# Attention steps on a fixed plan: one burst behind each second product instead of two paced streams

## The chip, the core and the metric

The kernel runs on one core of a Trainium2 chip. The metric is the time of one execution on the device, in microseconds (us); lower is better. Five engines work side by side, each through its own list of instructions in order: PE (TensorE, matrix products and transposes), DVE (VectorE), ACT (ScalarE), POOL (GpSimd) and SP (SyncE, which here issues nearly all DMA transfers). PE writes only to the accumulator memory PSUM, and DVE or ACT must empty a PSUM buffer before PE can use it again.

## The reference

Attention over 4 batches, 8 heads, 576 positions, 64 features per head, with two kinds of causal mask; then two MLPs over the 2304 tokens of width 512.

```python
mask_local = (rel >= 0) & (rel < 32)                       # heads 0 to 3
mask_strided = (rel >= 0) & (pos[None, :] % 32 == pos[:, None] % 32)   # heads 4 to 7
attn = softmax(where(mask, scale * q @ k.T, -1e9));  x = attn @ v       # -> (2304, 512)
h = x @ w_in;  r = np.maximum(h, 0.0);  x = (s * (r * r) + b) @ w_out   # d_ff = 2048
return ((x @ w_a) * (x @ w_b)) @ w_out2                                 # d_ff = 1536
```

## The kernel before

The tokens are cut into six blocks of 384 (`TB`), n = 0 to 5. For each block the first MLP runs over f = 0 to 15, slices of 128 hidden features. One iteration f has a **first product** `h_mm(n, f)` (12 matmuls of 128x384 into the PSUM tile `h`), whose result ACT and DVE turn into `gt`, and a **second product** `o_mm` for the slice two iterations back (12 matmuls into the four PSUM tiles `acc`). Every product is written as three passes over a high and a low half, so operands have a hi part (written by ACT) and a lo part (written by DVE, from the hi part).

A block's input tile `x` comes from attention, worked out while the block before it is in the MLP: during block n PE also does the attention of block n+1. Block 0's own attention (`first`) stands ahead of the loop. In block 0 DVE and ACT also convert the weights from raw words, one pair (`w_in`, `w_out`) per iteration, in `next_weights`; in blocks 1 to 4 they convert the second MLP's weights (`convert_w2`), which POOL stores to DRAM.

The attention of a block is four **local** generators (`local`, a pair of heads and 192 positions each) and two **strided** generators (`strided`, a pair of heads, in two halves); for block 1 it is four `strided_one` instead. A generator is a chain of steps separated by `yield`. The names in the trace, in the order of the chain:

- local: `pqk` (transposes of q and k; eight ACT copies into `qz` and `kT`), `pss` from `kT,qz` (scores), the softmax on `lpt` (DVE reduces and masks, ACT takes the exponentials, and a step later DVE normalises), `ppt` from `lpt` (transpose; ACT copies it to `pT`), `po` from `pT,vn` (output; ACT and DVE write it to `x`).
- strided: `pst` (transposes of q and k), `pss` from `skT,sqT`, softmax on `spt`, `ppt` from `spt`, `po` from `spT,sv`. `strided_one` is the same with the tile names `spo` and `spTo`.

The small tiles (`qn`, `kn`, `vn`, `kT`, `lpt`, `sk`, `sv`, ...) have one buffer each, and the attention's PSUM tiles share the three buffers of `ps_a`.

What sets the order: `in_order` chains every step's instructions behind PE's last one, so **PE's order is that of the code**. The other engines' lists are ordered by the framework's own scheduling, under that constraint. Two `Stream` objects, one for the local chain and one for the strided chain, are called twice in each iteration, once behind the first product and once behind the second (lines 810 to 816). A stream has a rate, steps divided by calls (line 701: `2 + 7 * len(gens)` steps, line 791: `2 * NF1 - 4` calls), and makes a step whenever a whole one is due; `overlapped` begins the next generator when the one before it is at its third or fourth step. So the places of the steps follow from the rates, and the two chains drift against each other.

At a block's end the four `acc` tiles are copied out by ACT (`o1s`, in three buffers shared with `r` and with each other) and stored by SP; the next block's second product needs those `acc` tiles from f = 2 on. When block 5 begins, the attention's pools are closed and SP loads the second MLP's first weights (`w` from `w2d`) and its input (`xr` from `o`, line 615) into the same memory. Some matmuls `pb` of the second MLP are then put between those of block 5.

Of the kernel before, what the change touches and what calls it, by code (L numbers as in the profile page):

```python
# [26 lines left out]
def sparse_attention_two_mlps(  # L27
# [28 lines left out]
    HL = H // 2  # L56
# [3 lines left out]
    TU = QT * NJ  # L60
# [4 lines left out]
    NB = NT // TB  # L65
    NT2 = TB // P
    KD = DM // P
    NF1 = FF1 // P
# [49 lines left out]
    @contextmanager  # L118
    def after(instructions):
        with ExitStack() as st:  # L120
            for i in instructions:
                st.enter_context(tc.issue_after(i))
            yield

    def in_order(step, *args):

        with after(list(last_pe)):
            return step(*args)
# [103 lines left out]
    def local(spans, n, hp_, c0):  # L232
# [39 lines left out]
        for j, (bb, t0) in enumerate(spans):  # L272
            nc.sync.dma_start(
                out=vn[:, j], in_=v[bb, hs, t0 - STR:t0 + QT, :].rearrange("h t d -> t h d")
            )
        yield
        pss = ps_a.tile([QT, 2, NJ, P], F32, tag="a", name="pss")
# [8 lines left out]
        yield from softmax(pt, [pss[:, i] for i in range(2)], mask[:, None, None, :].to_broadcast([QT, 2, NJ, P]))  # L286
        yield
        yield
# [104 lines left out]
    def strided(bb, pair):  # L393
# [29 lines left out]
        )  # L423
        yield
        half = S // QT // 2
# [6 lines left out]
        for g, r0 in enumerate(R0):  # L432
            for h in range(2):
# [3 lines left out]
                )  # L437
        yield
        kr = kT.rearrange("p (i r) -> p i r", r=STR)
        for g0, g1 in ((0, 3), (3, len(R0))):  # L440
# [11 lines left out]
            yield from softmax(pt, pss, smask[:, None, None, :].to_broadcast([NQ, 2, ng, NK]))  # L452
            yield
            yield
# [28 lines left out]
    def strided_one(pair, i):  # L483
# [22 lines left out]
        for j in range(2):  # L506
            for h in range(2):
# [3 lines left out]
                )  # L511
        yield
        pss = [ps_a.tile([QT, 2, TU], F32, tag="a", name="pss") for _ in range(2)]
        for j in range(2):
            for h in range(2):
                t = kqT[h * D:(h + 1) * D, 3 * j * QT:(3 * j + 3) * QT]
                mm(pss[h][:, j], lhsT=t[:, TU:], rhs=t[:, 0:TU], start=True, stop=True)
        pt = sp.tile([P, 2 * 3 * P], F32, tag="spt", name="spo")[:QT].rearrange("p (h j c) -> p h j c", h=2, j=2)
        yield from softmax(pt, pss, omask[:, None, None, :].to_broadcast([QT, 2, 2, TU]))
        yield  # L520
        yield
# [149 lines left out]

    def drain(gen):
        for _ in gen:
            pass

    class Stream:
# [10 lines left out]

    def overlapped(gens, at):

        next(gens[0])  # L690
        yield
        yield
        for i, g in enumerate(gens):
            for step, _ in enumerate(g):
                if step == at and i + 1 < len(gens):
                    next(gens[i + 1])
                yield

    def local_gens(n):
        if n == 1:  # L700
            spans = [[(2 * i, QT), (2 * i + 1, QT)] for i in range(2)]
        else:
            spans = [[(n - 2, p * TU), (n - 2, p * TU + QT)] for p in range(1, NP)]
        gens = [local(sp_, n, hp_, i * TU) for i, sp_ in enumerate(spans) for hp_ in range(HL // 2)]
        return overlapped(gens, 3), 2 + 7 * len(gens)

    def strided_gens(n):
        if n == 1:
            gens = [strided_one(pair, i) for i in range(2) for pair in range(2)]
            return overlapped(gens, 3), 2 + 7 * len(gens)  # L710
        gens = [strided(n - 2, pair) for pair in range(2)]
        return overlapped(gens, 4), 2 + 13 * len(gens)

# [61 lines left out]
    gens = [first(bb, qks[bb], vs[bb], fmask, *banks[bb]) for bb in range(B)]  # L775
    live, step = list(range(B)), 0
# [4 lines left out]
    for _ in range(EARLY):  # L781
        next_weights()
    later = [
        Stream(convert_w2(), 3 * NF2 + 1, (NB - 2) * NF1 - 2), Stream(column_sums(), NF1 + 1, 2 * NF1 - 1)
    ]
    queue = []
    for n in range(NB):
        acc = [ps_acc.tile([P, TB], F32, tag="acc", name="acc") for _ in range(KD)]
        if n + 1 < NB:

            streams = [Stream(*g(n + 1), 2 * NF1 - 4) for g in (local_gens, strided_gens)]
        else:
            streams = []
            att.close()
            p2 = ctx.enter_context(tc.tile_pool(name="p2", bufs=1, reuse_waits="tile"))
            wx = ctx.enter_context(tc.tile_pool(name="wx", bufs=NX, reuse_waits="tile"))
            for i in range(NX):
                load_w2(i)
            x2n = load_x2(0)
        for f in range(NF1):  # L800
            order = ExitStack()
            if n == 0:
                if len(wi) < NF1 and f:

                    with after(behind):
                        next_weights()

                order.enter_context(tc.issue_after(first_done[B - 1].ins))
            gt = in_order(h_mm, n, f)
            for st in streams:  # L810
                st()
            queue.append((acc, gt, f, n))
            if len(queue) > AHEAD1:
                in_order(o_mm, *queue.pop(0))
            for st in streams:
                st()
            order.close()
            if n == NB - 1:
                while len(w2) < NX + 2 * (f + 1 - AHEAD1):
                    load_w2(len(w2))  # L820
            elif n:
                for st in later[:n]:
                    st()
        for st in streams:
            drain(st.gen)
    for item in queue:
# [47 lines left out]
```

## Time and profile before

| | |
|---|---|
| median of 3 runs | 1040.44 us (1040.05 to 1041.5) |
| the profiled execution, its own time | 1042.37 us |
| the profiled execution, its span in the trace | 1040.5 us |
| PE busy | 997.3 us (96%) |
| weight loads of PE (PEld) busy | 936.0 us (90%) |
| DVE busy, ACT busy | 470.0 us (45%), 461.7 us (44%) |
| mean granted TensorE clock | 0.988 of full speed |

The span falls into stages: before the first `h` (to 39.4 us), block 0 (39.4 to 154 us), blocks 1 to 4 (154 to 511 us), block 5 and the second MLP (511 to 1040.5 us). In the timeline a row gives the start, the duration from the first to the last instruction of the group, the engine, line, tiles and count, and in brackets the idle time of the engine just before and what ended it. Matmuls overlap in the records, so what a group costs on PE is read from its start to the next group's start, not from its duration.

### The profile page before, as it was taken

Reading aid. Unit: us, or ns where it says so; the run is one execution under the profiler, and the core shown is the slowest. Engines: PE = TensorE matmul, PEld = TensorE weight load, DVE = VectorE, ACT = ScalarE, POOL = GpSimd, SP = SyncE. Lnnn points to the kernel's source line nnn. Section 1 sums busy time; section 2 is a strip of 40 time slices with the busy share of each in tenths; the row PEclk is TensorE's granted clock in tenths of the full one; section 3 lists DMA queues with packets and bytes.
Section 4 is the critical chain, followed back from the end, with each engine's and each line's share of the span. In section 5 each row is a group of like instructions: output and inputs, shape, how many; then the busy total and the mean of one; then the engine's idle time right before and its main releaser. Section 6 shows DMA issues by size and latency. Waiting matters only on the chain.

```text
span 1040.5 us, 15811 instructions
## 1 busy us (share of the span) xinstructions
PE 997.3 (96%) x5984; PEld 936.0 (90%) x5984; DVE 470.0 (45%) x1246; ACT 461.7 (44%) x1291; POOL 72.6 (7%) x110
## 2 busy tenths in 40 slices
PE   6878979999999899999999999999999999999998
PEld 5768979999899899889999989999999999999997
DVE  5689755766878677576522221211211211211111
ACT  6677846665675666567532231311311311211212
POOL 3000000001233132100000000000000000000000
PEclk9988989999999999999999999999999999999999
DMA  9556422456454554644567710200200100000000
GB/s 190 190 185 183 152 56 78 144 157 195 142 142 136 175 138 139 194 140 148 192 196 252 249 32 2 61 1 1 61 1 1 61 1 1 31 1 1 31 1 30
DMA packets 109819, 106.37 MB, mean 102 GB/s; under 512 B 59568, under 2 KB 94640, under 8 KB 109744
## 3 DMA queue, kind: packets, MB, share of 16 engines
q1 hardware_dynamic: 104560, 86.49, 28.9%
q0 software_dynamic: 5184, 18.88, 4.8%
q8 instruction: 47, 0.77, 0.3%
q14 instruction: 28, 0.23, 0.1%
HBM read 77.03 MB, written 28.31 MB: 101 GB/s over the span
## 4 chain that ended last, share of the span: by engine, by line
PE 85%; DVE 6%; ACT 5%; DMA 3%; issue 1%; SPq 0%; ACTq 0%; DVEq 0%
PE acc L113 30%; PE h L113 18%; PE pb L113 14%; PE pa L113 14%; PE pss L113 2%; PE po L113 2%; PE ppt L116 2%; DMA o<-o1s 1%; DMA xr<-o 1%; PE fss L113 1%; DVE raw L160 1%; DVE w L132 1%; DVE raw L163 1%; DVE raw L157 1%; ACT r L560 1%
## 5 line engine op out<-in xcount | busy, mean ns | idle before, releaser
L113 PE MATMUL h<-x,w 128*128 128x384 f32 x1152 | 229.2, 348 | 3.4 <-DVE w L132 1.3
L113 PE MATMUL acc<-gt,w 128*128 128x384 f32 x1152 | 223.0, 341 | 3.2 <-ACT o1s L586 3.2
L113 PEld LDWEIGHTS h<-x,w 128*128 128x128 f32 x1152 | 205.4, 194 | 7.9 <-DVE w L132 1.6
L113 PEld LDWEIGHTS acc<-gt,w 128*128 128x128 f32 x1152 | 199.4, 189 | 7.4 <-ACT o1s L586 3.8
L641 DVE TENSOR_TENSOR ab<-pb,ab 128x384 f32<-128x384 f32 x72 | 40.1, 557 | 306.7 <-ACT ab L640 306.7
L113 PE MATMUL pb<-x,w 128*128 128x384 f32 x864 | 165.0, 337 | 0.0
L113 PE MATMUL pa<-x,w 128*128 128x384 f32 x864 | 162.1, 335 | 1.5 <-ACT ab L640 1.5
L113 PE MATMUL acc<-w,abt 128*128 128x512 f32 x648 | 161.8, 393 | 0.0
L640 ACT ACTIVATE ab<-pa 128x384 f32<-128x384 f32 x72 | 35.4, 491 | 282.4 <-PE pa L113 282.3
L113 PEld LDWEIGHTS pb<-x,w 128*128 128x128 f32 x864 | 153.6, 188 | 6.4 <-DVE x L132 0.3
L113 PEld LDWEIGHTS pa<-x,w 128*128 128x128 f32 x864 | 150.8, 188 | 2.6 <-ACT ab L640 2.5
L113 PEld LDWEIGHTS acc<-w,abt 128*128 128x128 f32 x648 | 120.5, 188 | 21.9
L560 ACT ACTIVATE r<-h 128x384 f32<-128x384 f32 x96 | 46.8, 488 | 115.6 <-PE h L113 115.3
L567 DVE TENSOR_TENSOR r<-r 128x384 f32<-128x384 f32 x80 | 48.8, 610 | 91.1 <-ACT gt L566 90.5
L132 DVE TENSOR_TENSOR abt<-ab,abt 128x384 fp32r<-128x384 f32 x72 | 40.2, 558 | 46.8 <-ACT abt L131 46.8
L131 ACT ACTIVATE w<-raw 128x512 fp32r<-128x512 f32 x68 | 44.8, 670 | 25.7 <-DVE raw L163 21.6
L568 DVE TENSOR_TENSOR gt<-r,gt 128x384 fp32r<-128x384 f32 x80 | 54.1, 676 | 4.5
L132 DVE TENSOR_TENSOR w<-raw,w 128x512 fp32r<-128x512 f32 x68 | 45.9, 685 | 21.7 <-ACT w L131 20.8
L131 ACT ACTIVATE abt<-ab 128x384 fp32r<-128x384 f32 x72 | 37.7, 524 | 40.2 <-DVE ab L641 40.2
L604 POOL DMA_DIRECT2D w2d<-w x36 | 20.0, 556 | 431.6 <-DVE w L132 358.9
L163 DVE SCALAR_TENSOR_TENSOR raw<-raw 128x512 uint32<-128x512 uint32 x68 | 46.5, 686 | 0.7
L160 DVE SCALAR_TENSOR_TENSOR raw<-raw 128x512 uint32<-128x512 uint32 x68 | 45.9, 685 | 0.5
(109 smaller groups left out, 878.7 us busy)
## 6 DMA issues: line engine op xcount, KB each, us to landing
w2d<-w POOLq DMA_DIRECT2D x36, 512.0 KB, 5.2
w<-w2d SPq DMA_DIRECT2D x36, 512.0 KB
raw<-in_moe_w_out_dram SPq DMA_DIRECT2D x28, 512.0 KB
raw<-in_moe_w_in_dram SPq DMA_DIRECT2D x16, 512.0 KB
raw<-in_moe_w_a_dram SPq DMA_DIRECT2D x12, 512.0 KB
raw<-in_moe_w_b_dram SPq DMA_DIRECT2D x12, 512.0 KB
xr<-o SPq DMA_DIRECT2D x6, 768.0 KB
o<-o1s SPq DMA_DIRECT2D x20, 192.0 KB
```

The source lines that it names most:

```text
L113: last_pe[:] = [nc.tensor.matmul(*args, **kwargs).ins]
L116: last_pe[:] = [nc.tensor.transpose(*args).ins]
L131: nc.scalar.activation(out=hi, in_=src, func=AF.Copy)
L132: return eng_lo.tensor_tensor(out=lo, in0=src, in1=hi.bitcast(F32), op=ALU.subtract)
L160: nc.vector.scalar_tensor_tensor(out=low, in0=high, scalar=3, in1=low, op0=ALU.logical_shift_left, op1=ALU.bitwise_or)
L163: nc.vector.scalar_tensor_tensor(out=high, in0=high, scalar=0x80000000, in1=low, op0=ALU.bitwise_and, op1=ALU.bitwise_or)
L560: relu = nc.scalar.activation(out=r, in_=ph, func=AF.Relu)
L567: nc.vector.tensor_tensor(out=r, in0=r, in1=r, op=ALU.mult)
L568: lo = nc.vector.tensor_tensor(out=gt[:, 1], in0=r, in1=gt[:, 0].bitcast(F32), op=ALU.subtract)
L604: stores.append(nc.gpsimd.dma_start(out=w2d[i - 1], in_=w.bitcast(F32)).ins)
L640: nc.scalar.activation(out=ab, in_=pa, func=AF.Copy)
L641: nc.vector.tensor_tensor(out=ab, in0=pb, in1=ab, op=ALU.mult)
```

## The change

The streams, `overlapped` and the pacing by rate go. `plan(n)` lists for every generator the iteration numbers at which it makes its next step, and `attend(number)` makes all steps of one number. `attend` is called once per iteration, behind the second product; in the first three iterations of block 0, where steps would come too late, also behind the first product, and three numbers are called ahead of the loop. Numbers run on over the blocks, so the steps of one block's attention begin up to six iterations before the block in front of it and end in that block's last iteration.

```diff
-    def overlapped(gens, at):
-        next(gens[0])
...
+    steps = {}
+    def plan(n):
         if n == 1:
             spans = [[(2 * i, QT), (2 * i + 1, QT)] for i in range(2)]
+            far = [(4 * i - 3, strided_one(i % 2, i // 2), (-2, 0, 1, 2, 3, 4)) for i in range(4)]
         else:
             spans = [[(n - 2, p * TU), (n - 2, p * TU + QT)] for p in range(1, NP)]
+            far = [(8 * i - 3, strided(n - 2, i), (-3, 0, 1, 2, 3, 4, 4, 5, 6, 7)) for i in range(2)]
+        near = [
+            (4 * i - 1, local(spans[i // 2], n, i % 2, i // 2 * TU), (-2, 0, 1, 2, 3, 4)) for i in range(4)
+        ]
+        for first_, gen, at in near + far:
+            for t in at:
+                steps.setdefault((n - 1) * NF1 + first_ + t, []).append(gen)
+    def attend(number):
+        for gen in steps.pop(number, []):
+            in_order(next, gen)
...
             gt = in_order(h_mm, n, f)
-            for st in streams:
-                st()
+            if n == 0 and f < 3:
+                attend(2 * f - 3)
             queue.append((acc, gt, f, n))
             if len(queue) > AHEAD1:
                 in_order(o_mm, *queue.pop(0))
-            for st in streams:
-                st()
+            attend(n * NF1 + f if n or f > 2 else 2 * f - 2)
```

To fit, some `yield` lines go: the load of v is now in the step of the scores, the strided transposes of q and of k are one step, and of the two empty steps between the normalising and the transpose `ppt` one goes. The same instructions run; nothing in the work of a step changes.

PE at the start of block 0, before (`pss` from `skT` and `spo` belong to `strided_one`):

```order
L113 MATMUL h<-x,w 128x384 x24
L116 MATMUL pqk<-ident,qn 128x96 x2
L116 MATMUL pqk<-ident,kn 128x128 x2
L116 MATMUL pst<-ident,sk 128x96 x6
L113 MATMUL h<-x,w 128x384 x12
L113 MATMUL pss<-kT,qz 96x128 x4
L113 MATMUL pss<-skT 96x192 x4
L113 MATMUL acc<-gt,w 128x384 x12
L113 MATMUL h<-x,w 128x384 x12
L113 MATMUL acc<-gt,w 128x384 x12
L116 MATMUL ppt<-ident,lpt 128x96 x4
L116 MATMUL ppt<-ident,spo 96x96 x8
```

The same place after:

```order
L113 MATMUL h<-x,w 128x384 x12
L116 MATMUL pst<-ident,sk 128x96 x6
L113 MATMUL pss<-skT 96x192 x4
L113 MATMUL h<-x,w 128x384 x12
L116 MATMUL pqk<-ident,qn 128x96 x2
L116 MATMUL pqk<-ident,kn 128x128 x2
L113 MATMUL pss<-kT,qz 96x128 x4
L116 MATMUL ppt<-ident,spo 96x96 x8
L113 MATMUL h<-x,w 128x384 x12
L113 MATMUL po<-spTo,sv 64x96 x8
```

The strided chain has moved ahead of the local one and both begin earlier; transposes and the scores that read them now stand next to each other with no product between.

PE in block 1, iterations 5 to 7, before:

```order
L113 MATMUL h<-x,w 128x384 x12
L113 MATMUL pss<-skT,sqT 84x126 x4
L113 MATMUL acc<-gt,w 128x384 x12
L113 MATMUL pss<-kT,qz 96x128 x4
L113 MATMUL h<-x,w 128x384 x12
L113 MATMUL acc<-gt,w 128x384 x12
L116 MATMUL ppt<-ident,spt 126x84 x4
L113 MATMUL h<-x,w 128x384 x12
L116 MATMUL ppt<-ident,lpt 128x96 x4
L113 MATMUL po<-pT,vn 64x96 x4
L113 MATMUL po<-spT,sv 64x84 x4
L113 MATMUL acc<-gt,w 128x384 x12
```

PE in block 1, iterations 2 to 4, after:

```order
L113 MATMUL h<-x,w 128x384 x12
L113 MATMUL acc<-gt,w 128x384 x12
L116 MATMUL ppt<-ident,lpt 128x96 x4
L113 MATMUL h<-x,w 128x384 x12
L113 MATMUL acc<-gt,w 128x384 x12
L113 MATMUL po<-pT,vn 64x96 x4
L116 MATMUL pqk<-ident,qn 128x96 x2
L116 MATMUL pqk<-ident,kn 128x112 x2
L116 MATMUL ppt<-ident,spt 126x84 x4
L113 MATMUL h<-x,w 128x384 x12
L113 MATMUL acc<-gt,w 128x384 x12
L113 MATMUL pss<-kT,qz 96x128 x4
```

Before, `po` stands right behind the `ppt` it depends on; after, a whole pair of products lies between any two dependent steps. A block of 16 iterations has 23 such bursts before and 16 after, and no burst after uses more than three PSUM tiles of `ps_a`.

## Rows read from the trace of the kernel before

**Rows 1.** Busy time by stretch: us, then PE, PEld, DVE, ACT, POOL, clock, DMA.

```profile
39.40:154.00 114.60, 97.14 (x609) 90.37 (x610) 88.34 (x230) 82.14 (x218) 0.00 (x0) 0.91 0.47 144
70.40:142.80 72.40, 63.50 (x427) 59.58 (x426) 63.21 (x166) 57.18 (x156) 0.00 (x0) 0.90 0.44 131
154.00:511.00 357.00, 347.07 (x2401) 327.88 (x2400) 247.70 (x706) 228.67 (x728) 62.93 (x68) 1.00 0.50 149
```

**Rows 2.** Waits of PE in blocks 1 to 4: us in total, times, longest.

```profile
PE po L113 <- ACT pT L293: 3.6, 4, 1.2
PE acc L113 <- ACT o1s L586: 3.2, 2, 2.6
PE pst L116 <- ACT kT L267: 1.9, 4, 0.8
```

**Rows 3.** PE timeline in block 1, where nothing waits.

```profile
169.03 0.94 PE L113 MATMUL pss<-skT,sqT 64*84 64x126 f32 x12
169.90 2.38 PE L113 MATMUL h<-x,w 128*128 128x384 f32 x12
172.11 2.24 PE L113 MATMUL acc<-gt,w 128*128 128x384 f32 x12
174.19 0.49 PE L116 MATMUL ppt<-ident,lpt 96*128 96x96 f32 x4
```

**Rows 4.** ACT timeline: weight scaling in block 0, and four copies of transposes.

```profile
45.12 1.21 ACT L153 ACTIVATE raw<-raw 128x512 f32<-128x512 f32 x2
...
335.82 1.03 ACT L267 ACTIVATE qz<-pqk 64x96 f32<-64x96 f32 x4
```

**Rows 5.** PE timeline at the beginning of block 3.

```profile
346.20 0.79 PE L113 MATMUL acc<-gt,w 128*128 128x384 f32 x3 [2.59 <-ACT o1s L586]
...
348.41 3.22 PE L113 MATMUL h<-x,w 128*128 128x384 f32 x12
```

**Rows 6.** ACT and DVE timelines behind the last local output of block 4.

```profile
504.79 0.33 ACT L131 ACTIVATE x<-po 128x192 fp32r<-128x192 f32 x1
...
505.15 0.36 DVE L132 TENSOR_TENSOR x<-po,x 128x192 fp32r<-128x192 f32 x1 [0.95 <-ACT x L131]
```

**Rows 7.** Waits of the SP queue.

```profile
SPq L273 <- PE po L113: 93.3, 15, 12.0
```

**Rows 8.** Waits of PE in block 0.

```profile
PE ppt L116 <- DVE lpt L223: 7.6, 2, 5.4
PE ppt L116 <- DVE spo L223: 2.7, 1, 2.7
PE po L113 <- ACT pT L293: 2.0, 1, 2.0
PE po L113 <- DVE spTo L529: 1.4, 1, 1.4
PE h L113 <- DVE w L132: 1.3, 1, 1.3
PE pss L113 <- ACT kT L267: 1.1, 1, 1.1
```

**Rows 9.** PE timeline in block 0, at two of its waits.

```profile
69.23 1.49 PE L116 MATMUL ppt<-ident,spo 96*96 96x96 f32 x8 [2.69 <-DVE spo L223]
70.42 3.90 PE L113 MATMUL h<-x,w 128*128 128x384 f32 x12
...
140.88 0.87 PE L116 MATMUL ppt<-ident,lpt 96*128 96x96 f32 x4 [5.41 <-DVE lpt L223]
...
142.94 3.53 PE L113 MATMUL h<-x,w 128*128 128x384 f32 x12
```

**Rows 10.** Input of the second MLP: SP and ACT timelines, then the chain of waits.

```profile
504.78 0.37 SPq L615 DMA_DIRECT2D xr<-o  x1
...
516.16 2.14 ACT L620 ACTIVATE xr<-xr,b_col 128x384 f32<-128x384 f32 x4 [2.37 <-DMA w<-w2d]
...
604.27 4.46 DMA xr<-o
```

More of the change, by code (lines that the diff above doesn't have):

```diff
@@ L275, in local @@
             )
-        yield
         pss = ps_a.tile([QT, 2, NJ, P], F32, tag="a", name="pss")
@@ L286, in local @@
         yield from softmax(pt, [pss[:, i] for i in range(2)], mask[:, None, None, :].to_broadcast([QT, 2, NJ, P]))
-        yield
         yield
@@ L423, in strided @@
         )
-        yield
         half = S // QT // 2
@@ L437, in strided @@
                 )
-        yield
         kr = kT.rearrange("p (i r) -> p i r", r=STR)
@@ L452, in strided @@
             yield from softmax(pt, pss, smask[:, None, None, :].to_broadcast([NQ, 2, ng, NK]))
-            yield
             yield
@@ L511, in strided_one @@
                 )
-        yield
         pss = [ps_a.tile([QT, 2, TU], F32, tag="a", name="pss") for _ in range(2)]
@@ L519, in strided_one @@
         yield from softmax(pt, pss, omask[:, None, None, :].to_broadcast([QT, 2, 2, TU]))
-        yield
         yield
@@ L669, in token @@
         return (n - 2) * S + TU + c, TB
-    def drain(gen):
-        for _ in gen:
-            pass
     class Stream:
@@ L686, in __call__ @@
                 self.due -= 1.0
-    def overlapped(gens, at):
-        next(gens[0])
[L691 to L699, printed above, removed]
+    steps = {}
+    def plan(n):
         if n == 1:
             spans = [[(2 * i, QT), (2 * i + 1, QT)] for i in range(2)]
+            far = [(4 * i - 3, strided_one(i % 2, i // 2), (-2, 0, 1, 2, 3, 4)) for i in range(4)]
         else:
             spans = [[(n - 2, p * TU), (n - 2, p * TU + QT)] for p in range(1, NP)]
[L704 to L712, printed above, removed]
+            far = [(8 * i - 3, strided(n - 2, i), (-3, 0, 1, 2, 3, 4, 4, 5, 6, 7)) for i in range(2)]
[8 more added lines that the diff above has]
+            in_order(next, gen)
     AHEAD1, AHEAD2, EARLY = 2, 1, 3
@@ L785, in sparse_attention_two_mlps @@
     ]
+    for n in range(1, NB):
+        plan(n)
+    for number in (-6, -5, -4):
+        attend(number)
     queue = []
@@ L788, in sparse_attention_two_mlps @@
         acc = [ps_acc.tile([P, TB], F32, tag="acc", name="acc") for _ in range(KD)]
[L789 to L793, printed above, removed]
+        if n + 1 == NB:
+            assert not steps
             att.close()
@@ L823, in sparse_attention_two_mlps @@
                     st()
-        for st in streams:
-            drain(st.gen)
     for item in queue:
```

## The prediction, as it was made before the run

> **What bounds the kernel now.** I read the busy times by stretch first, then the waits of PE in each stretch, then the timelines around the longest of them. In blocks 1 to 4 PE works 347.1 of 357.0 us, at full clock, while DVE and ACT are busy 248 and 229 us [rows 1]: PE is the bound, and what a new order can give back there is the 9.9 us of idle PE and the price of switching between attention and products. Block 0 is another regime: PE 97.1 us, DVE 88.3 and ACT 82.1 us in 114.6 us, at a mean granted clock of 0.91 [rows 1]. Three engines are nearly full and wait for each other. From 511 us on there is no attention, and PE works nearly all the time; there I expect no gain.
>
> **Blocks 1 to 4, part by part.** *The waits.* 3.6 us are `po` waiting for ACT to copy `pT` [rows 2]: that happens where `ppt` and `po` stand in one burst. After the change 12 + 12 matmuls lie between them, two times 2.08 us by the starts of [rows 3] (172.11 to 174.19), against about half a microsecond for the copy. This wait goes, and so do 1.9 us of `pst` waiting for a PSUM buffer behind the copies of `kT` [rows 2], since no burst takes more than the three buffers and the next one comes 4.2 us later. In that time ACT has to make eight copies, of which four take 1.03 us [rows 4], so some 2.1 us of 4.2; together with the relu, the square and the weights there is still room. About 1.2 us of the 9.9 are small waits of other kinds, and they go with the spacing. The last 3.2 us are `acc` waiting at a block's beginning for the copies `o1s` [rows 2]. What ends them is a store out of the three shared buffers, and nothing in the plan speaks to that; it also cost clock: the `h` behind it lasted 3.22 us [rows 5] against 2.38 [rows 3], and the three matmuls and twelve scores ahead of that `h` took 2.2 us (346.20 to 348.41) instead of some 1.4; together 1.6 us. I count all 11.5 us as gone and put new waits against them: `o1s` again, between 0 and 4.2 us (2.6 + 1.6, its dearest case [rows 5]) at each of four block ends, and the new wait at a block's end. There the last local output now stands in the last iteration, right before the next block's first `h`, which reads it. The chain behind it is 0.33 us on ACT and 0.36 us on DVE, 0.72 us from 504.79 to 505.51 [rows 6], and the hand-over from PE; the transposes `pqk` behind it, some 0.4 us, and the first three matmuls of `h`, 0.5 us, cover most of that, so about 0.2 us if ACT and DVE are free and up to 1 us if not. Behind a waiting `h` everything on PE is queued. Together I take 4 us for the new waits, with ends 1 and 17.
>
> *The bursts.* The product behind a burst takes 2.21 us (169.90 to 172.11), the one behind a product 2.08 us (172.11 to 174.19) [rows 3]. That is 0.13 us per burst. Blocks 1 to 4 have 92 bursts before and 63 after (block 4 has one without): 29 x 0.13 = 3.8 us, take 4, with ends 2 and 6.
>
> *Work moved.* Transposes, six score pairs (169.03 to 169.90, 0.87 us [rows 3]) and `pqk` that began a block's attention now run in the block before: block 4 loses about 1.9 us, block 0 gains them.
>
> *The other queues.* A step carries its loads with it. Before, SP stood 93.3 us behind loads of v that waited for `po` to free the buffer [rows 7], with the weights and the stores of `o1s` queued behind them; after, `po` has read it an iteration earlier and SP passes. I count nothing for that, but it is the reason not to take the upper end for `o1s`. POOL's stores wait for DVE as before.
>
> Sum for blocks 1 to 4: -11.5 - 4 - 1.9 + 4 = **-13.4 us**.
>
> **Block 0.** *Its beginning.* The waits on PE up to 70.4 us are 2.2 (a part of the 7.6), 2.7, 1.3 and 1.1 us [rows 8], 7.3 in all. In their place come two chains with nothing in between. Behind `pst` the scores wait for a copy that stands on ACT behind the relu and two weight scalings of 1.21 us [rows 4]: about 1.2 us. Behind `pqk` the local scores wait for the eight copies, 2.1 us, and in ACT's list relu, square and weights stand among them: between 2.1 and 5.3 us, and I take 4.9, since all of those stand ahead. Those pieces then run at half clock, as the eight `ppt` at 69.23 did (1.19 us to the next start); some 2.3 us more. 4.9 + 1.2 + 2.3 - 7.3: **+1 us**, with ends -3 and +5.
>
> *The rest.* From 70.4 us PE waits 2.0 + 1.4 + 5.4 us [rows 8], and each longer wait costs clock behind it: `h` lasted 3.90 us at 70.42 and 3.53 us at 142.94 [rows 9], against 2.38 [rows 3]. That makes some 12 us that could come back. But the weights must be converted: from 70.4 to 142.8 us, where the last one is ready, DVE was busy 63.2 of 72.4 us [rows 1], so the last weight cannot come more than 9 us earlier, and each engine still waits for another now and then. The softmax now has a whole iteration more before `ppt` reads it, which is what the 5.4 us lacked. I take **-8 us**, ends -12 and +3. The moved work adds 1.9, fewer bursts take 1 off. Block 0: +1 - 8 + 0.9 = **-6 us**.
>
> **Block 5.** The last local output comes one iteration later against the block's beginning, and the load of `xr` waits for it. Before, it was issued at 504.78 and used at 516.16, behind 2 MB of weights [rows 10]; after, those weights wait for the strided tiles only, which are free three iterations earlier, and `xr` alone lands in 4.46 us [rows 10]. `pb` stands where it stood, behind the second iteration's `acc`. I take **+1 us**, ends 0 and +8.
>
> **Sum:** -13.4 - 6 + 1 = -18.4. The profiled execution took 1042.37 us with a span of 1040.5, 1.9 us around it; it would take 1024.0. Against the median of the runs, 1040.44, that is **1022 us**.
>
> **Rivals.** (a) *Block 0 gives nothing.* DVE's weights stay the bound there and every gap closed on PE opens as a wait for a weight: then -13.4 + 1 give **1028**. For it: DVE 63.2 of 72.4 us; against it: PE waited once for a weight in the whole block, 1.3 us [rows 8]. Chance 0.12. (b) *Block ends.* `o1s` costs 4.2 us at each of four ends [rows 5]: 17 instead of 4, **1035**. For it: the plan does not touch its cause, and exponentials now stand in ACT's list beside the copies; against it: in two of the four ends it cost nothing before. Chance 0.06. (c) *The input of the second MLP* is late: if `xr` again needs 11.4 us, but from the beginning of block 5, the `pb` matmuls wait and the products behind them too, +8: **1029**. Chance 0.04. (d) *The clock.* The bursts gather transposes, and their rows show no loss so far: clock 1.00 in blocks 1 to 4 [rows 1], where six to nine transposes and small score groups already stood before a product. If a burst left the clock at its lower level, 1.2 GHz, the `h` behind it would take 3.2 instead of 2.2 us [rows 5]; for the seven bursts of nine transposes plus their neighbours about 8 us: **1030**. The Trainium skill, TensorE: Matmul & The Clock Gate, Part 4 (PE-mode transpose), says that transposes do not count as activity of PE for the clock in the way matmuls do, which speaks for this rival; the clock of 1.00 here does not bear it out. Chance 0.03. (e) *Slower.* In block 0 a burst uses all three PSUM buffers, and the next one needs them 4.2 us of products later. If DVE, with the weights in its list, is later than that with the reduce of the scores, PE waits in every burst until the thirteenth: 13 waits of 2.0 us, like the one for `pT` [rows 8], are 26 us, and nothing of the 8 us comes back: -13.4 + 1 + 0.9 + 26 + 1 = +15.5 give **1056** at worst; without the 26 the sum is -10.5, so it decides for slower from 10.5 / 13 = 0.8 us per burst. For it: DVE is 87% busy in that stretch [rows 1]; against it: before, PE never waited there for a reduce [rows 8]. With some 1.1 us per burst it is 1044. Chance 0.12, a quarter of it within the noise. That the change does not do what it says is excluded by the order of PE's instructions.
>
> **How the numbers follow.** The forecast (1010 to 1027) has 0.63; (a) to (d) have 0.25 and are faster too; (e) has 0.12. A difference of under 0.2% (2 us) is about what a measurement here cannot tell from no change. Faster 0.87, within it 0.04 (0.03 of (e), 0.01 of (b)), slower 0.09. For the range I leave out (e) and the lowest 0.05 of the forecast: 1010 to 1035.
>
> **What would show it.** Right: blocks 1 to 4 in some 343 us with `po`-behind-`pT` and `pst`-behind-`kT` gone from the waits of PE; block 0 in about 108 us, with a wait of several us for `kT` near its beginning and no 5 us wait for `lpt`; block ends with waits of under 1 us for `x`. Wrong: waits of PE for a reduce of `mx` or for weights in block 0, waits for `o1s` at every block end, a granted clock under 1.00 in blocks 1 to 4, or `pb` or `h` waiting for `xr` at the beginning of block 5.

## The result, and the profile after

The changed kernel takes 1023.84 us (median of 4 runs, 1022.7 to 1027.23) where the kernel before took 1040.24 us beside it: 0.985 of the time, 95% interval 0.9826 to 0.9874, 16.4 us less. The prediction was 1022 us. Run again later, on a chip where the kernel before took 1040.1 us, it took 1024.1 us: 0.9849 (0.983 to 0.9868). The profiled execution took 1023.17 us with a span of 1021.4 us, against 1042.37 and 1040.5 us.

The blocks are told apart by where each block's first `h` begins in PE's timeline. The table gives the profiled executions, and the sums that the prediction had made.

| stretch | before, us | after, us | difference | predicted |
|---|---|---|---|---|
| block 0 | 114.5 | 106.1 | -8.4 | -6 |
| blocks 1 to 4 | 86.55 + 87.82 + 93.80 + 88.91 = 357.1 | 85.13 + 87.77 + 89.16 + 85.32 = 347.4 | -9.7 | -13.4 |
| block 5 and the second MLP | 529.5 | 528.6 | -0.9 | +1 |
| sum | | | -19.0 | -18.4 |

The sum was nearly right and its parts were less so. The first view is busy time by stretch, as in [rows 1] with its columns (us, PE, PEld, DVE, ACT, POOL, clock, DMA): first of the kernel before with the cuts at the blocks' first `h`, then of the changed kernel.

```profile
39.45:153.94 114.49, 97.08 (x608) 90.31 (x609) 88.23 (x230) 82.14 (x218) 0.00 (x0) 0.91 0.47 143
153.94:511.02 357.08, 347.15 (x2401) 327.96 (x2401) 247.78 (x706) 228.67 (x728) 62.93 (x68) 1.00 0.50 149
511.02:1040.50 529.48, 523.20 (x2785) 493.28 (x2784) 109.42 (x201) 123.92 (x250) 0.00 (x0) 1.00 0.17 54
```

```profile
39.36:145.44 106.08, 95.90 (x634) 88.36 (x634) 91.17 (x245) 84.48 (x233) 0.00 (x0) 0.97 0.52 158
145.44:492.82 347.38, 341.85 (x2378) 324.37 (x2377) 251.55 (x689) 225.57 (x713) 63.30 (x68) 1.00 0.52 154
492.82:1021.40 528.58, 522.96 (x2786) 493.41 (x2784) 109.50 (x201) 124.47 (x251) 0.00 (x0) 1.00 0.16 53
```

PE's idle time, the stretch less PE's busy time, fell from 17.4 to 10.2 us in block 0 and from 9.9 to 5.5 us in blocks 1 to 4. In block 0 PE issued 26 matmuls more and in blocks 1 to 4 23 fewer: that is the first attention of block 2, which moved forward. It is counted among what blocks 1 to 4 save and what block 0 must carry.

PE's waits after, in us, times and the longest, which answer to [rows 8] (block 0) and to [rows 2] (blocks 1 to 4). First block 0:

```profile
PE pss L113 <- ACT kT L267: 4.9, 1, 4.9
PE ppt L116 <- DVE lpt L223: 2.2, 1, 2.2
PE pss L113 <- ACT skT L387: 1.0, 1, 1.0
PE pst L116 <- ACT sqT L419: 1.0, 1, 1.0
...
```

and blocks 1 to 4:

```profile
PE h L113 <- ACT r L553: 4.0, 4, 1.8
PE h L113 <- DVE x L132: 1.1, 2, 0.7
PE h L113 <- ACT x L131: 0.2, 1, 0.2
```

No wait for `pT`, none of `pst` for a buffer behind `kT` and none of `acc` for `o1s` is left. The 5.4 us wait for `lpt` near the end of block 0 [rows 9] is gone. What is there instead is one long wait at the beginning of block 0, for `kT`, and waits of `h` for the relu `r`, a kind that the prediction had not named.

The 1.0 us of `pst` corrects the description of the change, which says that no burst takes more than three PSUM tiles of `ps_a`. One does, in block 0, where the last steps of block 1's attention meet the first of block 2's: the output `po`, the transposes `pst` of q and the two halves of those of k want four tiles, and the last half waits until ACT has copied `sqT` out of one. PE's timeline:

```profile
131.83 0.93 PE L113 MATMUL po<-spTo,sv 96*64 96x96 f32 x16
132.70 0.55 PE L116 MATMUL pst<-ident,sq 128*128 128x128 f32 x3
133.08 0.41 PE L116 MATMUL pst<-ident,sk 96*128 96x96 f32 x3
134.45 0.47 PE L116 MATMUL pst<-ident,sk 96*128 96x96 f32 x3 [0.96 <-ACT sqT L419]
```

### The profile page after: what moved, and what is told of

Its sections match the earlier page's. It is cut to its first block, busy times and chain, and to the rows that moved or that the text cites. A ratio compares the mean times of both kernels' runs of the same rounds, so it can differ in the third digit from the quotient of the medians.

```text
span 1021.4 us, 15787 instructions
## 1 busy us (share of the span) xinstructions
PE 990.5 (97%) x5984; PEld 930.6 (91%) x5984; DVE 476.8 (47%) x1246; ACT 461.6 (45%) x1291; POOL 73.0 (7%) x110
## 4 chain that ended last, share of the span: by engine, by line
PE 72%; ACT 10%; DVE 10%; DMA 4%; issue 2%; POOL 0%; SPq 0%; ACTq 0%; POOLq 0%; DVEq 0%
PE acc L113 25%; PE pb L113 14%; PE pa L113 14%; PE h L113 13%; DVE gt L561 2%; DMA w2d<-w 2%; DVE raw L160 2%; PE pss L113 2%; ACT w L131 1%; ACT raw L153 1%; DVE w L132 1%; DMA o<-o1s 1%; DVE raw L157 1%; ACT spt L216 1%; DMA xr<-o 1%
## 5 line engine op out<-in xcount | busy, mean ns | idle before, releaser
L113 PE MATMUL acc<-gt,w 128*128 128x384 f32 x1152 | 215.6, 334 | 0.0
L113 PEld LDWEIGHTS h<-x,w 128*128 128x128 f32 x1152 | 200.7, 191 | 15.4 <-ACT r L553 5.4
L561 DVE TENSOR_TENSOR gt<-r,gt 128x384 fp32r<-128x384 f32 x80 | 60.5, 756 | 4.0
```

What stands on the lines that cost most here:

```text
L113: last_pe[:] = [nc.tensor.matmul(*args, **kwargs).ins]
L561: lo = nc.vector.tensor_tensor(out=gt[:, 1], in0=r, in1=gt[:, 0].bitcast(F32), op=ALU.subtract)
```

## The experiments

Every ratio is to the kernel before, run beside it on the same chip. The changed kernel stands at 0.985.

**1. The plan in block 0 alone.** Do the two gains stand by themselves?

```
-    for n in range(1, NB):
-        plan(n)
+    plan(1)
...
+        if 0 < n < NB - 1:
+            streams = [Stream(*g(n + 1), 2 * NF1 - 4) for g in (local_gens, strided_gens)]
```

> The planned steps are kept for what runs in block 0 (the attention of block 1's columns, behind the first 16 pairs of products); blocks 1 to 4 run their attention from the two streams of the kernel before, with the yields put back. Theory: the two gains are separate. Block 0 then takes about 104 us (106.1 in the changed kernel less the 1.9 us of later attention that it had taken in; 114.5 before), blocks 1 to 4 about 357 us as before with their waits for pT, kT and o1s back at about 9 us, the whole about 1030 us. Rival: part of the gain of block 0 rests on the first steps of the later attention lying in it, or hands its waits to block 1: then block 1 begins later or is longer than 86.5 us, and the whole is 1033 to 1037 us.

Measured: 1032.71 us, 0.9923 (0.9909 to 0.9937). Block 0 took 104.2 us in the profile and blocks 1 to 4 358.5 us, 86.84 + 89.19 + 93.61 + 88.89. The waits of blocks 1 to 4 are back by name; this is the view of PE's waits up to 500 us:

```profile
PE po L113 <- ACT pT L295: 4.5, 5, 1.2
PE acc L113 <- ACT o1s L586: 2.9, 2, 2.3
PE pst L116 <- ACT kT L267: 1.9, 4, 0.8
```

So the gains are separate: block 0 keeps all of its gain without the later plan (104.2 is 106.1 less the moved 1.9 us), and blocks 1 to 4 give theirs only if they are planned themselves. The time is a little above the theory, since block 2 took 1.4 us more than before.

**2. Two bursts per pair.** What does it cost to switch between attention and products?

```
-            for t in at:
-                steps.setdefault((n - 1) * NF1 + first_ + t, []).append(gen)
+                for t in at:
+                    steps.setdefault(((n - 1) * NF1 + first_ + t, k), []).append(gen)
...
+            if n or f > 2:
+                attend(n * NF1 + f, (0,))
```

> Same steps under the same numbers, but a number's local step stands behind the first product and its strided step behind the second, so a block has 32 short bursts of attention where the changed kernel has 16 and the kernel before 23. This prices the bursts alone. Theory: a burst costs 0.09 us (what block 1 gained without its waits, 0.62 us for 7 bursts), 16 more in each of blocks 1 to 4 and about 14 in block 0 are 78 x 0.09 = +7 us, less the 1.3 us of waits for x at the block ends, since the local output is ready half a pair earlier: about 1029 us. By the 0.13 us of the prediction it is +10 - 1.3, 1032 us. Rival: the number of bursts costs nothing, and the gain came from the spacing and from what runs side by side: 1022 us.

Measured: 1025.68 us, 0.986 (0.9844 to 0.9875), whose interval overlaps that of the changed kernel. By PE's timeline there are 24 bursts in a block, not the 32 expected: steps that only load or copy put nothing on PE. That is 8 more than in the changed kernel, one more than before. Block 1, where neither kernel has a wait, prices them:

```profile
147.10:232.49 85.39, 85.39 (x600) 80.95 (x599) 53.27 (x167) 55.84 (x180) 3.99 (x7) 1.00 0.49 140
```

85.39 against 85.13 us is 0.26 us for 8 bursts, 0.03 us each. The prediction had 0.13. The row of the trace was right, but it was not the price of a burst. By PE's starts in block 1, the 32 products take 70.0 us here against 68.8 in the changed kernel, 0.15 us more for each further burst; but the same 214 small matmuls take 15.4 us against 16.3. Groups that follow each other in one burst cost something between them too, and a cut between them gives most of that back. Block 2 took 85.38 us (no wait for the relu), block 3 89.90 with a wait of 1.2 us for a buffer, and block 0 1.6 us more than in the changed kernel; behind block 4 another 2.2 us went, with `pb` waiting 1.1 us for a load of weights. With one burst a block more than the kernel before, blocks 1 to 4 take 346.5 us here, nearly the time of the changed kernel: **the number of bursts is not where the gain came from.**

**3. The scaled sum out of the relu's buffers.** What ends the waits of `h` for `r`? The wait of 1.80 us stands at the fourth pair of block 2. PE's timeline of the changed kernel (start, us, what, idle before it and its releaser), and ACT's there:

```profile
244.01 2.25 PE L113 MATMUL acc<-gt,w 128*128 128x384 f32 x12
246.09 0.49 PE L116 MATMUL ppt<-ident,lpt 96*128 96x96 f32 x4
248.39 2.35 PE L113 MATMUL h<-x,w 128*128 128x384 f32 x12 [1.80 <-ACT r L553]
```

```profile
247.85 0.49 ACT L553 ACTIVATE r<-h 128x384 f32<-128x384 f32 x1 [1.98 <-DMA o<-o1s]
```

`h` has one PSUM buffer, so a product waits until the relu of the pair before has read it. The page's name for the wait stops at the relu; ACT's row goes one link further: the relu stood idle 1.98 us for a DMA, the store of `o1s`, which holds one of the three buffers of tag `r`. The first of the block's four stores, issued at 241.14 us, had landed 1.95 us later; the second, which the relu waited for, was issued at 242.02 and landed 5.7 us later. Between the two stands a 512 KB load of weights in SP's queue:

```profile
241.14 0.35 SPq L580 DMA_DIRECT2D o<-o1s  x1
241.60 0.38 SPq L139 DMA_DIRECT2D raw<-in_moe_w_b_dram  x1
242.02 3.07 SPq L580 DMA_DIRECT2D o<-o1s  x3
```

POOL issued a 512 KB store of its own at 241.68 us as well, and no run separates the two. The place in SP's queue is not the whole of it: in block 4 the second store was issued at 418.59, ahead of SP's load at 419.22, and landed 4.3 us later, with POOL's store issued at 418.74.

The edit gives the scaled sum another place, the `x` of the block that has just ended, where it is rounded to the shorter type of `x`:

```
-            o = hp.tile([P, TB], F32, tag="r", name="o1s", bufs=3) if last is None else last[:, e]
+            o = x_t[n][:, 0, e, :] if last is None else last[:, e]
...
-            nc.sync.dma_start(out=o1[e * P:(e + 1) * P, cols], in_=o)
+            nc.sync.dma_start(out=o1[e * P:(e + 1) * P, cols], in_=o.bitcast(F32) if last is None else o)
```

> At a block's end the scaled sum is put into the x of the block that has just ended instead of the three buffers that it shares with the relu (it is rounded to the shorter type of x there, so the stored values are rounded; nothing else is left out). Theory 1: the relu of pair 3 waits for the store of the scaled sum that holds its buffer; in the changed kernel ScalarE sat idle 1.98 us ahead of it at 247.85 us, released by that DMA. Then the 1.80 us that the product waits at 248.39 goes and the time is about 1.8 us less, 1021 to 1022 us. Theory 2: the other three waits for the relu in blocks 1 to 4 (0.68, 0.77 and 0.79 us) have no DMA in them; ScalarE runs exponentials up to the relu's start. They stay. Rival: all four come from the buffers, and 4 us go, 1019 us; or the wait moves to the next link and nothing goes.

Measured: 1019.21 us, 0.9797 (0.9784 to 0.9811): 0.5% under the changed kernel, where theory 1 expected 0.2%. Blocks 1 to 4 took 344.0 us instead of 347.4: block 2 lost 2.0 us, block 4 1.0 and block 3 0.3. In block 2 the relu now follows the exponentials at once:

```profile
244.91 0.47 ACT L553 ACTIVATE r<-h 128x384 f32<-128x384 f32 x1
```

Theory 2 fell for block 4. There the relu at 425.00 had indeed only exponentials ahead of it, but those stood behind two copies that had waited for the stores of their own block, two links further back. ACT's timeline of the changed kernel:

```profile
420.21 0.58 ACT L579 ACTIVATE o1s<-acc,sb 128x384 f32<-128x384 f32 x1 [0.37 <-DMA o<-o1s]
422.99 0.58 ACT L579 ACTIVATE o1s<-acc,sb 128x384 f32<-128x384 f32 x1 [2.20 <-DMA o<-o1s]
423.47 0.39 ACT L216 ACTIVATE spt<-spt,mx 84x126 f32<-84x126 f32 x1
...
425.00 0.47 ACT L553 ACTIVATE r<-h 128x384 f32<-128x384 f32 x1
```

In block 3 theory 2 held: one wait for the relu, 1.5 us, stays. The profile accounts for 3.4 us of span; the runs say 0.5% (4.6 us by the two medians). Some 1 us of that is not placed.

**4. The first transposes one place forward.** Is the 4.9 us wait at the beginning a matter of order?

```
-    for number in (-6, -5, -4):
+    for number in (-6, -5, -4, -3):
...
-                attend(2 * f - 3)
+                for number in ((-2, -1), (0,), (1,))[f]:
+                    attend(number)
...
-            attend(n * NF1 + f if n or f > 2 else 2 * f - 2)
+            if n or f > 1:
+                attend(n * NF1 + f)
```

> The steps at the beginning are drawn one place forward: the number -3 stands ahead of the first product, -2 and -1 behind pair 0's first product, 0 behind pair 1's, 1 behind pair 2's, so the transposes of the first keys are followed by a pair of products before the scores want kT. Theory: the wait of 4.92 us for kT (and 1.01 us for skT) comes from transposes and scores standing one short product apart while ScalarE still converts weights; with more between them most of it goes and the time is 3 to 5 us less, about 1019 to 1020 us. Rival: ScalarE and VectorE are the bound of the beginning (conversion of the weights), so what the scores no longer wait for, a later step or the products wait for: within 1 us of the changed kernel.

Measured: 1019.45 us, 0.9802 (0.9786 to 0.9817). Block 0 took 101.4 us instead of 106.1. PE's timeline, first of the changed kernel, then of this one:

```profile
51.26 0.38 PE L116 MATMUL pqk<-ident,kn 128*128 128x128 f32 x2
56.57 2.01 PE L113 MATMUL pss<-kT,qz 128*96 128x128 f32 x8 [4.92 <-ACT kT L267]
...
59.56 2.55 PE L113 MATMUL h<-x,w 128*128 128x384 f32 x12
```

```profile
45.73 0.39 PE L116 MATMUL pqk<-ident,kn 128*128 128x128 f32 x2
45.87 2.34 PE L113 MATMUL h<-x,w 128*128 128x384 f32 x12
51.05 1.51 PE L113 MATMUL pss<-kT,qz 128*96 128x128 f32 x8 [2.84 <-ACT kT L267]
54.46 1.51 PE L116 MATMUL ppt<-ident,spo 96*96 96x96 f32 x8 [1.89 <-DVE spo L223]
```

With one `h` between the transposes and the scores the wait is 2.84 us, and the wait for `skT` is gone. A new one for `spo` takes 1.89 us, and still the third pair's first product begins 3.9 us earlier (55.68 against 59.56 us). The rival that ACT and DVE bound the beginning holds for what remains of the waits, not for the 4.7 us.

**5. The output behind its own transposes.** Is it the spacing, then?

```
-            (4 * i - 1, local(...), (-2, 0, 1, 2, 3, 4)) for i in range(4)
+            (4 * i - 1, local(...), (-2, 0, 1, 2, 3, 3)) for i in range(4)
```

> Of each local group the product that makes the output stands in the same burst as the transposes of its probabilities, where the changed kernel puts it one burst later; all else stays. This prices the spacing. Theory: what the change removed are waits of TensorE for a copy on ScalarE, and a pair of products between two steps is what covers them. Without it TensorE waits, in 20 bursts, for the transposes (0.5 us), ScalarE's turn and its copy of pT (0.49 us): 1.2 to 2.1 us each (the copy began up to 2.1 us behind the transposes at 424.24 us), +24 to +42 us, less 1.3 us of waits for x at the block ends that go: 1046 to 1065 us, and the waits for pT are there by name. Rival: the gain comes from fewer bursts or from work that moved, and the copy is quick enough: 1022 to 1028 us.

Measured: 1030.36 us, 0.9922 (0.9903 to 0.9941). The waits come back by name and in the number foreseen. The waits of PE in the whole trace, and PE's timeline at one of them:

```profile
PE po L113 <- ACT pT L291: 13.2, 20, 2.0
```

```profile
161.45 0.49 PE L116 MATMUL ppt<-ident,lpt 96*128 96x96 f32 x4
162.52 0.55 PE L113 MATMUL po<-pT,vn 128*64 128x96 f32 x8 [0.58 <-ACT pT L291]
163.00 2.35 PE L113 MATMUL h<-x,w 128*128 128x384 f32 x12
```

Twenty waits, 0.66 us in the mean instead of the 1.2 to 2.1 expected, since ACT mostly came to the copy at once where I had taken a late case. Block 1 shows the price bare: 87.46 against 85.13 us, 2.33 us for four waits of 0.58. The `h` behind keeps its 2.35 us. Blocks 1 to 4 lost 5.3 us: 10.8 us of these waits, less 3.5 us by which the waits for `r` and `x` shrank and 2.0 us of PE busy time. So spacing this one step is worth 0.7% of the time within the plan, as much as nearly half of the change's gain and more than the bursts. The kernel before had five such waits, not twenty, of 5.6 us in all (3.6 [rows 2] and 2.0 [rows 8]). The two sums are near each other, but this run prices the step within the plan, not what the change took from the kernel before.

**6. The local heads one pair earlier.** Is it the shift?

```
-            (4 * i - 1, local(...), (-2, 0, 1, 2, 3, 4)) for i in range(4)
+            (4 * i - 2, local(...), (-2, 0, 1, 2, 3, 4)) for i in range(4)
```

> The local heads' steps all stand one pair earlier against the strided ones; each group's own spacing stays. This tests the shift between the two. The steps of the two kinds share three PSUM tiles; in the changed kernel no burst wants more than three, here about 3 of every 8 want four. Theory: in those TensorE waits within the burst until VectorE or ScalarE has read a tile, some 1 us each, 6 a block in blocks 1 to 4, 24 to 30 in all: +10 to +30 us, 1034 to 1054 us. Rival: the tile that is read first comes free in time, and as the waits for x at the block ends go the time is 1.3 us less, 1022.5 us.

Measured: 1047.72 us, 1.008 (1.0057 to 1.0104): slower than the kernel before, as the theory said, by one number in the plan. Block 0 took 114.2 us and blocks 1 to 4 361.8 us. There are fewer waits than expected, but they cost more. PE's timeline in block 2, and the busy times behind the wait:

```profile
249.05 0.49 PE L116 MATMUL ppt<-ident,lpt 96*128 96x96 f32 x4
249.47 0.66 PE L113 MATMUL po<-spT,sv 126*64 126x84 f32 x12
250.06 0.66 PE L113 MATMUL pss<-skT,sqT 64*84 64x126 f32 x4
252.18 0.66 PE L113 MATMUL pss<-skT,sqT 64*84 64x126 f32 x4 [1.46 <-ACT pT L291]
252.76 3.39 PE L113 MATMUL h<-x,w 128*128 128x384 f32 x12
255.95 2.86 PE L113 MATMUL acc<-gt,w 128*128 128x384 f32 x12
```

```profile
252.70:255.90 3.20, 3.20 (x14) 3.14 (x13) 2.05 (x10) 2.15 (x10) 2.42 (x3) 0.68 0.58 153
```

`ppt`, `po` and the first scores hold the three PSUM tiles, and the fourth tile, for the second half of the scores, is the one that the copy of `pT` frees. PE waits 1.46 us, and the two products behind it take 3.39 and 2.86 us at a mean granted clock of 0.68 in the first: 1.65 us over the usual 2.35 and 2.25, so this wait costs twice its length. Of the five waits for a tile or for `o1s` in blocks 2 to 4, four take 1.4 to 1.5 us, with an `h` of 3.39, 3.92, 3.45 and 3.29 us behind them; the fifth takes 0.84 us, and the `h` behind it 2.35. In block 0 the longest wait is one of 6.4 us for the sum of the exponentials, near where the changed kernel waits 4.9 us for `kT`.

**7. The last burst of a block behind its first product.**

```
+            if f == NF1 - 1:
+                attend(n * NF1 + f)
```

> Only the last burst of each block, which makes the last quarter of the next block's x, stands behind the pair's first product instead of its second. Theory: the waits for x at the ends of blocks 2 and 3 (0.21 + 0.39 and 0.74 us) and of block 4 go, about 1.3 to 2 us: 1022 us. Rival: ScalarE and VectorE have the same queue there (the weight conversion, the relu's split), x comes as late, or the products behind the burst meet the scaled sum on ScalarE, as the 1.6 us in a kernel with two bursts per pair: within 1 us of the changed kernel, 1023 to 1025 us.

Measured: 1022.22 us, 0.9838 (0.9823 to 0.9852): 0.1% under the changed kernel, which these runs can't tell from none. In its profile blocks 1 to 4 took 343.6 us instead of 347.4. The waits for `x` shrank to 0.3 us as in the theory, but block 2, where there had been none, lost the most (2.2 us): there the scaled sum's first two stores (239.61 and 240.49 us) now stood ahead of both the 512 KB load in SP's queue (242.62) and POOL's store (242.89), and the relu no longer waited for them. The edit met the wait of experiment 3 by chance. Behind block 4 it lost 1.2 us again. The profiled execution's gain (2.5 us of span) and that of the runs (1.2 us by the ratios) differ, so its size stays open.

**8 to 10. Together.** The edits of 3 and 4; those two and that of 7; and the changed kernel beside the latter.

> The scaled sum in the dead x (its stored values are rounded to the shorter type) together with the first transposes one place forward. Theory: the two gains lie in different blocks, 3.4 us in blocks 1 to 4 and 5.2 us in block 0 and the span's end by their profiles, 4.6 and 4.4 us by their times; they add up: 1014 to 1015.5 us. Rival: part of either is the time of day of transfers that the other moves too: 1016 to 1018 us.

> The three edits together: the scaled sum in the dead x (rounded there to its shorter type), the first transposes one place forward, and the last burst of a block behind the pair's first product. Theory: the x waits that are left in blocks 2 to 4 (1.6 us, with the buffers mended) go and nothing takes their place, since the scaled sum no longer holds a buffer that the relu wants: 1.2 to 1.6 us under the kernel with the first two edits, 0.976 of the kernel before, 1014 to 1016 us. Rival: the gain of the third edit was the same wait for the relu at pair 3 that the first edit had already removed (block 2 went from 87.77 to 85.53 us with either): nothing is left but block 4's 0.7 us, 1016 to 1017 us.

> The changed kernel itself, on the same chip as the kernel with the three edits, so that the two stand side by side. Its time by the ratio of the first comparison, 0.985 of the kernel before: 1023 to 1025 us where that takes 1038.5 to 1040.2 us.

Measured: with two edits 1015.58 us, 0.9777 (0.9762 to 0.9793); with three 1015.74 us, 0.9765 (0.9747 to 0.9782); the changed kernel again 1024.1 us, 0.9849. Each of the first two gave about 0.5%, together they give 0.73% of the kernel before. With intervals of 0.13 to 0.24% either way on each ratio, that cannot be told from their sum, so whether they add up in full stays open. In the profile block 0 takes 102.5 and blocks 1 to 4 343.2 us with two edits, 3.6 and 4.2 us less than in the changed kernel. The third edit brings nothing that can be told: the intervals overlap, and the times fit its theory and its rival. By the profiles the waits for `x` did shrink from 1.3 to 0.3 us, but waits of 0.5 to 1.0 us for the relu and for a reduce took their place in blocks 3 and 5, where the theory had expected none. The version with three edits is 8.4 us faster than the changed kernel on the same chip and 24.4 us faster than the kernel before, at the price of an output of the first MLP that is stored in the shorter type's precision.

## Why the prediction was right, and where its terms were not

The step from waits to a plan, the place of each gain and the sum were right; three terms were mis-sized, and that their errors cancelled is luck.

*Waits of blocks 1 to 4* (-11.5). Right. The 9.9 us of idle PE went under their old names, and the clock's 1.6 us came back: block 3, the only one with a clock under 1.00 before, has 1.9 us less PE busy time (89.03 to 87.11), which holds the price of its 8 fewer bursts too. Experiment 5 shows the mechanism for `pT`: where spacing is undone, the wait is there.

*New waits* (+4). Mis-sized: PE's idle time in these blocks is 5.5 us. At the block ends `x` takes 1.3 us, as foreseen (0.2 to 1 us each). For `o1s` I had kept a wait of `acc` [rows 5]; no `acc` waited. The store of `o1s` still held a buffer, and the wait went to the next that wanted one, the relu, and through it to `h`: 4.0 us, of which experiment 3 removed 2.5.

*Bursts* (-4). Mis-sized: PE's busy time in blocks 1 to 4 fell by 5.3 us, of which 1.6 are clock and 1.9 are work that moved; 1.8 us are left for 29 bursts, 0.06 each; experiment 2 gives 0.03, and block 1 alone, net of its waits, 0.09. The step that failed was to read the price of a burst from the product behind it [rows 3] without asking what the groups within a burst cost each other: in block 1 the products take 0.9 us less than before (68.8 against 69.7), 0.13 us for each of 7 bursts as predicted, and the small matmuls without their waits 0.3 us more (16.3 against 16.0).

*Work moved* (-1.9, +1.9). Right: block 0 is 1.9 us shorter where it does not carry that work (experiment 1). The four terms then add up to what was measured, -9.9 - 1.6 - 1.8 - 1.9 + 5.5 = -9.7 us, but the clock's 1.6 is the prediction's own figure and the bursts' 1.8 is what was left over.

*Block 0, the beginning* (+1). The two waits came as worked out, 4.92 us for `kT` (4.9 taken) and 1.01 for `skT` (1.2 taken). That the first fits so closely is luck: in the second profile of the changed kernel and in those of experiments 1, 2, 3, 5 and 7, which all begin alike, it is 5.9 us, above the upper end that the prediction gave (5.3). The third `acc` began at 75.45 us before and at 74.27 us after, with the first `h` at 39.45 and 39.36, so the beginning gave 1.1 us instead of costing 1. In the second profile it took 35.6 us (38.11 to 73.73), 0.4 us less than before, so even the sign is not safe. The mis-sized term is the slow clock, +2.3 us: PE's busy time up to there grew by 0.7 us only (27.5 to 28.2), with 18 matmuls more in it. The beginning had slow stretches before as well that I had not credited, this `h` in the timeline of the kernel before among them:

```profile
45.28 4.21 PE L113 MATMUL h<-x,w 128*128 128x384 f32 x12 [0.58 <-ACT r L560]
```

Busy time of the stretches up to and from the third `acc`, before and after:

```profile
39.40:75.45 36.05, 27.50 (x147) 24.64 (x147) 27.14 (x66) 23.88 (x60) 0.00 (x0) 0.91 0.53 172
75.45:153.94 78.49, 69.59 (x464) 65.67 (x463) 61.13 (x164) 58.26 (x159) 0.00 (x0) 0.91 0.44 131
```

```profile
39.40:74.27 34.87, 28.24 (x165) 25.47 (x166) 25.91 (x71) 24.36 (x70) 0.00 (x0) 0.95 0.57 178
74.27:145.44 71.17, 67.62 (x471) 62.85 (x470) 65.22 (x175) 60.12 (x164) 0.00 (x0) 0.98 0.49 149
```

*Block 0, the rest* (-8 + 1.9 - 1 = -7.1). Right in size: 78.5 us from 75.45 on before, 71.2 us here, -7.3. What in the plan gives it was not taken apart: block 0 keeps nearly all of its gain without the spacing of `po` (106.7 us, experiment 5) and loses it with the shift (114.2 us, experiment 6). Rival (a), DVE's weights as the bound, did not come, though DVE is busy 65.2 of 71.2 us; nor did rival (e): there is no wait for a reduce in the changed kernel (the 2.2 us for `lpt` are for the multiplication behind it). The kernel with the shift (experiment 6) is slower than before, but not by the 13 waits of (e): in block 0 one wait of 6.4 us for a sum stands out, and in blocks 2 to 4 waits for a fourth tile.

*Block 5* (+1). It is 0.9 us shorter. `xr` was issued at 492.97, the addition that reads it began at 497.54, and `pb` began at 501.47 without a wait: rival (c) did not come.

*Clock* (rival (d)). Blocks 1 to 4 kept 1.00, so a burst with nine transposes did not lower it by itself. The rival's price also set a duration (3.2 us) against a distance of starts (2.2); by durations [rows 3, rows 5] it is 3.22 against 2.38 us.

## What to carry to other kernels

Small dependent steps beside a stream of long products should be placed by hand so that a whole product lies between a step and the copy that the next one reads, and so that no burst wants more buffers than there are; how many bursts there are hardly mattered here (0.03 to 0.09 us each). Before a wait is counted as gone, find what ends it: a buffer held by a store makes the next user wait when the first one no longer does, and mending that gave another third of what the change had given. Follow a wait past the instruction that the page names, to what that engine itself waited for.

## What was not expected of the hardware

A wait of PE does not cost the same everywhere. In the changed kernel `h` waited 1.80 us at 248.39, behind 24 matmuls of products and four transposes, and then took its usual 2.35 us at a clock of 1.00. With the local heads shifted, 1.46 us among 24 short matmuls left a clock of 0.68, and two products lost 1.65 us. In the same kernel `acc` waited 1.49 us for `o1s` right ahead of a burst, and the `h` behind took 3.92 us:

```profile
347.40 0.79 PE L113 MATMUL acc<-gt,w 128*128 128x384 f32 x3 [1.49 <-ACT o1s L579]
...
349.31 3.92 PE L113 MATMUL h<-x,w 128*128 128x384 f32 x12
```

It is tempting to conclude that a wait within a burst of short matmuls is the dear one, but the other runs do not bear that out. In experiment 5 a longer wait stands within a burst, and the product behind it keeps its usual length:

```profile
338.83 0.55 PE L113 MATMUL po<-pT,vn 128*64 128x96 f32 x8 [1.99 <-ACT pT L291]
339.31 2.38 PE L113 MATMUL h<-x,w 128*128 128x384 f32 x12
```

And at one place of block 0, where `h` waits for a weight with ten of its matmuls left, these ten took 2.02 us behind a wait of 0.96 us in experiment 4, and 3.54 us, at a clock of 0.50, behind a wait of 0.93 us in the kernel with two edits. So a wait of 1 to 2 us sometimes cost as much again and sometimes nothing; what decides it is not shown here.

Also, executions of one kernel differ at the beginning: the second profile of the changed kernel shows two waits for `kT`, of 5.9 and 1.0 us, instead of one of 4.9, a clock of 0.77 instead of 0.95 up to the third `acc`, and block 0 in 106.5 us instead of 106.1.
